# Clustered attention with a Mish feed-forward layer: another form for three tiny products, loads of V set apart, and a new order of issue

## The chip, the cores and the metric

One NeuronCore of a Trainium2 chip runs the whole kernel. The metric is the device time of one execution in microseconds (us). The engines are TensorE (PE, matrix products), VectorE (DVE), ScalarE (ACT), GpSimd (POOL) and the queue of SyncE (SP), which issues most DMAs. Each engine works through its own instructions in order, and so does each queue.

## The reference: attention inside clusters, then a feed-forward layer

```python
q_n, k_n, c_n = (t / (norm(t) + 1e-6) for t in (q, k, centroids))
q_assign = argmax(einsum('bhsd,hcd->bhsc', q_n, c_n))   # 16 clusters
k_assign = argmax(einsum('bhsd,hcd->bhsc', k_n, c_n))
mask   = q_assign[:, :, :, None] == k_assign[:, :, None, :]
scores = where(mask, q @ k.T / sqrt(64), -1e9)          # 768 x 768 per head
attn   = softmax(scores)
x = (attn @ v), heads side by side                       # (3072, 512)
h = x @ w_in                                             # (3072, 2048)
out = (h * tanh(softplus(h))) @ w_out                    # (3072, 512)
```

There are 4 batches of 8 heads, 768 positions and 64 numbers per head.

## The kernel before

**Units of work.** A unit `i` is one head and one block of 256 queries, so there are 96 units, 24 for each batch; each has two halves `a` of 128 queries. For a half, `scores(i, a)` (lines 625 to 643) writes 128 x 768 scores to PSUM, `rowmax` (L648, DVE) takes the row maxima, `expo` (L662, ACT) the exponentials with their sums, `total` and `recip` (L674, L682, DVE) the reciprocal sums. There are two PSUM buffers for scores, so `scores` of one half waits until `expo` two halves before has read its own.

From unit 24 on, the probabilities are split into two half-precision parts: `p_hi` on POOL (L700) and `p_lo` on DVE (L717: a scalar-tensor-tensor, which reads two tensors from SBUF). `ptrans` (L733) transposes both by DMA on SP's queue, and `pv(m, part)` (L753, PE) multiplies the transposed probabilities of units 2m and 2m+1 with V. In the first 24 units PE transposes instead (L710), and V is used in full precision. `pv_out` and `x_lo` (L790, L814) bring the result to SBUF. `prep_hi` and `prep_lo` (L484, L487, L500; POOL) split the next head's q and k; `prep_lo` is a tensor-tensor.

**Feed-forward layer.** `m1` (L832 to L834), `e_mish` (L843, ACT), `e_gh` (L849, POOL), `e_gl` (L857, DVE) and `m2` (L873 to L875) run between the units of the batch that follows. Weights are loaded, scaled and split in the first 200 us (`w_load`, `w_low`, `w_f32`, `w_sq`, `w_hi`, `w_lo`).

**V and the scales.** V of batch b comes in four loads of 384 KB, `v_load(b, hp)` (L356, SP's queue), one per two heads. The loads and the split copies that `v_high` (L441, POOL) and `v_split` (L430, DVE) make share six buffers. `v_sq` (L368, ACT) squares each load for the batch's scale. A scale per batch is a power of two in a 128 x 1 column. `moe_scale_h(b)` (L447, L451) and `moe_scale_o(b)` (L459) multiply such columns on DVE, once per batch: twelve instructions in all, each on 128 x 1 numbers.

**What sets the order.** Every operation has a due time, made from the tables `T`, `N` and, one operation at a time, `SHIFT` (line 41). The planner (line 51) issues them by due time; `pl.after` in an operation first issues what it needs. All engines and SP's queue then keep that order, so an operation that waits holds whatever stands behind it on its engine or queue.

Of the kernel before, what the change touches and what calls it, by code (L numbers as in the profile page):

```python
# [72 lines left out]
def tile_clustered_attention_mish_ffn(  # L73
# [1327 lines left out]
    ('load', 0): -8.977,  # L1401
    ('load', 1): -9.331,
    ('load', 2): -6.804,
    ('load', 3): -5.619,
    'prep_hi': -3.465,
    'prep_lo': 0.23,
    'copy_t': -2.657,
    'copy_z': -2.269,
    'copy_a': -1.819,
    'hot_copy': -1.496,  # L1410
    'copy_b': -0.963,
    'assign_mm': -3.945,
    'assign_turn': -4.253,
    'assign_max': -4.024,
    'assign_hot': -0.819,
    'assign_back': -3.241,
    'assign_put': 1.027,
    'assign_stg': -2.392,
# [11 lines left out]
    'expo': 3.967,  # L1430
    'total': 8.731,
    'recip': 0.231,
    'p_hi': 3.325,
    'p_lo': 4.618,
    'ptrans': 0.814,
    'pv': [3.293, 11.429, 2.946],
    'pv_out': 7.913,
    'x_lo': 2.788,
    'm1': [0.115, 0.891, 1.22, 1.321],
    'e_mish': [7.039, 1.656],  # L1440
    'e_gh': [1.735, 2.085],
    'e_gl': [1.659, 2.922],
    'm2': [5.418, 4.348, 9.247, 4.881, 6.012, 11.05, 9.763, 4.899, 4.471, 5.038, 4.927, 19.283, 4.585, 5.024, 8.214, 4.739],
    'm_out': -0.192,
    'm_store': -0.425,
# [10 lines left out]
    ('qk_load', 1): 0.234, ('qk_load', 2): -8.097, ('qk_load', 3): 0.234, ('w_f32', 29): 0.56, ('w_low', 18): 0.238,
    ('w_low', 22): -0.008, ('pv', 5, 0): 0.03, ('w_low', 19): -0.127, ('pv_out', 10): 6.683, ('v_split', 1, 1): 0.53,
    ('recip', 8, 1): 0.054, ('recip', 1, 1): 0.532, ('w_hi', 10): -0.025, ('rowmax', 18, 1): 0.004,
    ('total', 7, 1): 0.207, ('w_low', 29): 0.382, ('w_low', 31): 0.354, ('total', 14, 1): 0.631, ('w_load', 0): 0.812,
    ('p_hi', 7, 0): 0.769, ('p_hi', 6, 1): -0.119, ('p_hi', 6, 0): 0.699, ('w_low', 21): 0.177, ('pv', 11, 0): 0.16,  # L1460
    ('w_f32', 17): -0.125, ('p_hi', 0, 0): -0.048, ('p_hi', 0, 1): -0.024, ('p_hi', 1, 0): -0.518,
    ('p_hi', 1, 1): -0.022, ('p_hi', 2, 0): -0.009, ('p_hi', 2, 1): -0.009, ('p_hi', 3, 1): -0.009,
    ('p_hi', 4, 1): -0.009, ('p_hi', 5, 1): -0.009, ('expo', 16, 1): 1.76, ('expo', 10, 1): -2.352,
    ('total', 11, 1): 2.886, ('p_lo', 20, 1): -0.478, ('p_lo', 21, 1): -0.062, ('p_lo', 22, 0): -0.335,
    ('p_lo', 22, 1): 0.969, ('p_lo', 23, 0): 0.043, ('p_lo', 23, 1): -0.838, ('p_lo', 24, 0): 2.44,
    ('p_lo', 24, 1): -0.148, ('p_lo', 25, 0): -1.539, ('p_lo', 25, 1): 1.12, ('p_lo', 26, 0): -0.755,
    ('p_lo', 27, 0): 0.027, ('scores', 29, 0): -0.211, ('rowmax', 21, 0): -0.09, ('v_sq', 0, 3): -0.653,
    ('w_load', 5): -0.533, ('e_gh', 0): -0.048, ('e_gh', 1): -0.048, ('copy_z', 9): -0.31, ('copy_z', 10): -0.069,
    ('copy_a', 8): -0.101, ('copy_a', 9): -0.042, ('w_low', 11): 0.141, ('rowmax', 5, 0): 0.002,
    ('v_load', 1, 3): -0.147, ('w_load', 6): 0.218, ('copy_z', 0): -0.468, ('prep_lo', 6): 6.254,  # L1470
# [5 lines left out]
    ('p_hi', 19, 1): 0.777, ('p_hi', 20, 0): 0.068, ('p_hi', 20, 1): 0.068, ('p_hi', 21, 0): 0.128,
    ('p_hi', 21, 1): 0.118, ('p_hi', 22, 0): 1.691, ('p_hi', 22, 1): 0.068, ('p_hi', 23, 0): 0.029,
    ('p_hi', 23, 1): 0.713, ('copy_b', 6): 0.145, ('copy_b', 7): 0.475, ('copy_b', 9): 0.03, ('centroids',): -0.486,
    ('x_lo', 12): 0.064, ('scores', 14, 0): 0.142, ('p_lo', 2, 1): -0.108, ('copy_t', 0): 0.443,
# [169 lines left out]
```

## Time and profile before

| | |
|---|---|
| median of 3 runs | 874.17 us (872.82 to 874.46) |
| the profiled execution, its own time | 873.21 us |
| its span (what the trace covers) | 871.5 us |
| PE busy | 839.7 us, 96% of the span |
| DVE, ACT, POOL busy | 698.3, 517.1, 437.9 us |
| granted TensorE clock | 1.0 (2.4 GHz) |

The profile gives, for one execution, busy time by engine and stretch, what ended each idle time, and every instruction with its start. 1.7 us of the profiled time lie outside the span.

### The profile page before, as it was taken

The page shows a single profiled execution, that of the slowest core. Times are in us where ns is not written, and L with a number is a line of the kernel's source. Part 1 is how long each engine was busy: PE and PEld are TensorE (multiplying, and loading weights), DVE is VectorE, ACT ScalarE, POOL GpSimd, SP SyncE. Part 2 cuts the span into 40 slices and gives each one's busy share as a digit, 9 for nine tenths or more (in the row PEclk, how much of TensorE's full clock was granted, in tenths as well). Part 3 has the DMA queues.
Part 4 walks back from the last instruction along what each step waited for, and adds up shares of the span by engine and source line. Part 5 has one row for each costly group of instructions (what it writes and reads, how often), then busy time and mean ns, then how long its engine had stood idle before and what let it go on. Part 6 is the DMA issues. An engine that isn't in the chain of part 4 may idle for free.

```text
span 871.5 us, 17410 instructions
## 1 busy us (share of the span) xinstructions
PE 839.7 (96%) x6671; PEld 608.6 (70%) x6671; DVE 698.3 (80%) x1178; ACT 517.1 (59%) x878; POOL 437.9 (50%) x410
## 2 busy tenths in 40 slices
PE   7899899889999999999999999999999999999998
PEld 3666666667767767776677767776776776777787
DVE  7889988889978878779978789779888776488831
ACT  6778977667547567456556666465565565245520
POOL 1463655486657646556567457466557543110000
PEclk9999999999999999999999999999999999999999
DMA  9755671289679897698679897987877976000000
GB/s 333 240 176 160 186 219 48 63 163 186 132 136 180 207 169 146 130 190 168 124 128 200 189 172 132 156 178 149 142 136 135 156 130 118 23 1 14 2 31 32
DMA packets 253060, 121.51 MB, mean 139 GB/s; under 512 B 230288, under 2 KB 230800, under 8 KB 252976
## 3 DMA queue, kind: packets, MB, share of 16 engines
q1 hardware_dynamic: 247632, 108.46, 59.4%
q10 hardware_dynamic: 5344, 11.93, 6.6%
q8 instruction: 53, 0.87, 0.4%
q14 instruction: 31, 0.25, 0.1%
HBM read 35.72 MB, written 6.29 MB: 48 GB/s over the span
## 4 chain that ended last, share of the span: by engine, by line
PE 72%; DVE 12%; DMA 5%; ACT 4%; POOL 3%; issue 3%; ACTq 0%; SPq 0%; DVEq 0%; POOLq 0%
PE o L753 9%; PE h L832 8%; PE h L834 8%; PE h L833 8%; PE O L873 7%; PE O L875 7%; PE O L874 7%; PE s L631 5%; PE s L636 5%; DVE m L648 4%; DMA pt<-hl 3%; DVE hl L717 2%; ACT p L662 2%; PE as L543 1%; PE q L710 1%
## 5 line engine op out<-in xcount | busy, mean ns | idle before, releaser
L662 ACT ACTIVATE p<-s,m 128x768 f32<-128x768 f32 x192 | 172.7, 899 | 174.2 <-DVE m L648 94.7
L700 POOL TENSOR_SCALAR hl<-p,l 128x768 f16<-128x768 f32 x144 | 172.7, 1200 | 149.3 <-DVE l L682 82.3
L648 DVE TENSOR_REDUCE m<-s 128x1 f32<-128x768 f32 x192 | 182.5, 952 | 39.7 <-PE s L636 36.2
L832 PE MATMUL h<-x,w 128*128 128x256 f16 x640 | 175.8, 275 | 2.5 <-ACT u L843 2.0
L717 DVE SCALAR_TENSOR_TENSOR hl<-p,l,hl 128x768 f16<-128x768 f32 x144 | 166.6, 1157 | 12.8 <-POOL hl L700 12.5
L833 PE MATMUL h<-x,w 128*128 128x256 f16 x640 | 174.4, 273 | 0.0
L834 PE MATMUL h<-x,w 128*128 128x256 f16 x640 | 174.4, 273 | 0.0
L631 PE MATMUL s<-A,B 128*128 128x384 f32 x384 | 118.9, 391 | 7.1 <-ACT p L662 6.1
L873 PE MATMUL O<-w,g 128*128 128x512 f16 x320 | 121.7, 380 | 0.0
L875 PE MATMUL O<-w,g 128*128 128x512 f16 x320 | 121.3, 379 | 0.0
L874 PE MATMUL O<-w,g 128*128 128x512 f16 x320 | 121.3, 379 | 0.0
L857 DVE SCALAR_TENSOR_TENSOR g<-u,mscg,g 128x512 f16<-128x512 f32 x80 | 91.6, 1145 | 34.2 <-POOL g L849 34.0
L849 POOL TENSOR_SCALAR g<-u,mscg 128x512 f16<-128x512 f32 x80 | 75.0, 940 | 65.7 <-ACT u L843 53.2
L636 PE MATMUL s<-Z,T 80*128 80x384 f32 x384 | 99.0, 339 | 2.2 <-DMA T<-stg 1.2
L832 PEld LDWEIGHTS <-w 128*128 128x128 f16 x768 | 75.1, 98 | 30.9 <-issue 19.7
L833 PEld LDWEIGHTS <-w 128*128 128x128 f16 x768 | 75.5, 98 | 13.9 <-issue 2.7
L753 PE MATMUL o<-pt,v 128*64 128x256 f16 x1296 | 79.1, 274 | 3.5 <-DMA pt<-hl 3.5
L834 PEld LDWEIGHTS <-w 128*128 128x128 f16 x768 | 75.1, 98 | 9.0 <-issue 0.2
L753 PEld LDWEIGHTS <-v 128*64 128x64 f16 x1296 | 68.4, 110 | 15.6 <-issue 11.7
L631 PEld LDWEIGHTS s<-A,B 128*128 128x128 f32 x384 | 61.3, 190 | 21.5 <-ACT p L662 9.4
L636 PEld LDWEIGHTS s<-Z,T 80*128 80x128 f32 x384 | 69.5, 189 | 3.0 <-DMA T<-stg 1.5
L500 POOL TENSOR_TENSOR B<-qk,A 128x768 fp32r<-128x768 f32 x30 | 61.6, 2052 | 0.6
(225 smaller groups left out, 1299.0 us busy)
## 6 DMA issues: line engine op xcount, KB each, us to landing
qk<-in_qk_dram SPq DMA_DIRECT2D x32, 384.0 KB, 4.8
stage<-in_w_in_dram SPq DMA_DIRECT2D x16, 512.0 KB, 6.6
stage<-in_w_out_dram SPq DMA_DIRECT2D x16, 512.0 KB, 4.4
vraw<-in_vP_dram SPq DMA_DIRECT2D x16, 384.0 KB, 6.2
T<-A ACTq DMA_DIRECT2D x30, 192.0 KB, 3.5
Z<-B SPq DMA_DIRECT2D x30, 192.0 KB, 3.0
B<-T ACTq DMA_DIRECT2D x28, 192.0 KB, 3.4
out_dram<-osb SPq DMA_DIRECT2D x20, 256.0 KB, 2.7
```

The lines of the kernel that those rows point to most:

```text
L631: nc.tensor.matmul(s[:, j, :384], st["B", n][:, q0 : q0 + P], st["A", n][:, j * 384 : (j + 1) * 384], start=True, stop=False,)
L636: nc.tensor.matmul(s[:, j, :384], st["T", n][: D + NCL, q0 : q0 + P], st["Z", n][: D + NCL, j * 384 : (j + 1) * 384], start=False, stop=True,)
L648: nc.vector.tensor_reduce(m, st["s", i, a][:, :, :384], axis=AX.XY, op=ALU.max, negate=True)
L662: nc.scalar.activation(p.rearrange("p (n x) -> p n x", n=2), st["s", i, a][:, :, :384], AF.Exp, bias=st["m", i, a], scale=1.0, accum_out=l,)
L717: nc.vector.scalar_tensor_tensor(t[:, 1], p, r, t[:, 0], op0=ALU.mult, op1=ALU.subtract)
L753: nc.tensor.matmul(o[s * D : s * D + D, :256], v if early else v[:, int(part == 1)], st["pt", 2 * m + s][:, :, c + (0 if early or part < 2 ...
L832: nc.tensor.matmul(o, wh, xh, start=(c == 0), stop=False)
L833: nc.tensor.matmul(o, wh, xl, start=False, stop=False)
L834: nc.tensor.matmul(o, wl, xh, start=False, stop=(c == 3))
L873: nc.tensor.matmul(o, gh, wh, start=(f == 0 and fi == 0), stop=False)
L874: nc.tensor.matmul(o, gh, wl, start=False, stop=False)
L875: nc.tensor.matmul(o, gl, wh, start=False, stop=(f == 7 and fi == 1))
```

## The change

Three things, in one diff. The products of columns in `moe_scale_h` and `moe_scale_o` become tensor-scalar instructions whose second column is a per-partition scalar operand. The loads of V of batches 2 and 3, whose four due times were equal, get due times of their own, from 0.6 to 6.6 units earlier. And the tables of due times are new: some 100 entries of `T` and `N`, and `SHIFT` grows from 705 entries, nearly all in the first 32 units, to 2,524 over the whole kernel. Shares, buffers and the work itself stay.

```diff
     def moe_scale_h(b):
         pl.after(scaled(b), ("w_scale", 0))
         t = sm.tile([P, 1], F32, tag="msch", name=f"msch{b}")
-        nc.vector.tensor_tensor(t, vst[b, "s"][:, 1:2], wst["s", 0][:, 1:2], op=ALU.mult)
+        nc.vector.tensor_scalar(t, vst[b, "s"][:, 1:2], wst["s", 0][:, 1:2], None, op0=ALU.mult)
         vst[b, "h"] = t
...
-        nc.vector.scalar_tensor_tensor(
-            g, vst[b, "s"][:, 0:1], 2.0**-14, wst["s", 0][:, 0:1], op0=ALU.mult, op1=ALU.mult
+        nc.vector.tensor_scalar(
+            g, vst[b, "s"][:, 0:1], wst["s", 0][:, 0:1], 2.0**-14, op0=ALU.mult, op1=ALU.mult
         )
...
     def moe_scale_o(b):
...
-        nc.vector.scalar_tensor_tensor(
-            t, vst[b, "h"], 2.0**14, wst["s", 1][:, 1:2], op0=ALU.mult, op1=ALU.mult
+        nc.vector.tensor_scalar(
+            t, vst[b, "h"], wst["s", 1][:, 1:2], 2.0**14, op0=ALU.mult, op1=ALU.mult
         )
...
 N = {
-    'v_load': 17.351,
+    'v_load': 16.905,
...
 SHIFT = {
+    ('v_load', 2, 0): -6.115, ('v_load', 2, 1): -4.014, ('v_load', 2, 2): -1.835, ('v_load', 2, 3): -0.275,
+    ('v_load', 3, 0): -6.141, ('v_load', 3, 1): -5.728, ('v_load', 3, 2): -2.038, ('v_load', 3, 3): -0.148,
...
```

(The last lines put together entries that stand apart in the new table.) Sorted by due time, each operation behind what it needs, the two tables give two orders. Counted in stretches of one operation, PE has 907 of which 789 keep their order among themselves; DVE 894 of 1,062, ACT 529 of 637, POOL 307 of 370, SP's queue 249 of 314. Nearly all moves are over at most four places. SP's queue around V of batch 2, before and after:

```
before: ... ptrans(39,1) hot_copy(14) ptrans(40,0) qk_load(18) v_load(2,0) v_load(2,1) v_load(2,2) v_load(2,3) ptrans(40,1) ptrans(41,0) ptrans(41,1)
after:  ... v_load(2,0) ptrans(34,0) ... v_load(2,1) ptrans(36,0) ... v_load(2,2) ptrans(38,0) ... ptrans(39,1) v_load(2,3) ptrans(40,0) qk_load(18) ptrans(40,1) qk_load(17) ptrans(41,0) ptrans(41,1)
```

## Rows read from the trace of the kernel before

**Rows 1.** Busy time by stretch: PE, PEld, DVE, ACT, POOL, clock, DMA share, GB/s.

```profile
0.00:200.00 200.00, 177.18 (x1335) 124.21 (x1336) 176.77 (x322) 148.86 (x282) 105.83 (x125) 1.00 0.62 177
200.00:750.00 550.00, 544.26 (x4371) 389.77 (x4369) 450.50 (x738) 322.28 (x526) 324.65 (x278) 1.00 0.82 153
```

**Rows 2.** Timeline of DVE around 161 us: start, us, line, operation.

```profile
161.20 2.11 DVE L447 TENSOR_TENSOR msch<-vs0r,ws0r 128x1 f32<-128x1 f32 x1
...
163.30 0.94 DVE L648 TENSOR_REDUCE m<-s 128x1 f32<-128x768 f32 x1
```

**Rows 3.** Timeline of POOL around 161 us.

```profile
161.16 2.13 POOL L349 TENSOR_TENSOR w<-w,w 128x1024 f16<-128x1024 f32 x1
```

**Rows 4.** Timeline of PE around 165 us; in brackets the idle time before.

```profile
165.39 0.62 PE L631 MATMUL s<-A,B 128*128 128x384 f32 x2 [1.00 <-ACT p L662]
```

**Rows 5.** One line, L447: its last execution, ns shortest, median, longest.

```profile
L447 DVE TENSOR_TENSOR msch<-vs3r,ws0r x1: 147/147/147, 733.9 to 733.9; 128x1 f32<-128x1 f32 x1
```

**Rows 6.** Timeline of DVE around 350 us.

```profile
350.03 1.76 DVE L447 TENSOR_TENSOR msch<-vs1r,ws0r 128x1 f32<-128x1 f32 x1
...
351.78 1.00 DVE L717 SCALAR_TENSOR_TENSOR hl<-p,l,hl 128x768 f16<-128x768 f32 x1
```

**Rows 7.** Timeline of POOL around 350 us.

```profile
349.53 2.24 POOL L500 TENSOR_TENSOR B<-qk,A 128x768 fp32r<-128x768 f32 x1
```

**Rows 8.** One line, L674: ns shortest, median, longest, and its shapes.

```profile
L674 DVE TENSOR_SCALAR l<-l x146: 133/144/585, 115.5 to 732.0; 128x1 f32<-128x1 f32 x144, 128x2 f32<-128x2 f32 x2
```

**Rows 9.** Timeline of DVE: the longest L674, and L610 with its column operand `put_b`.

```profile
71.95 1.02 DVE L610 TENSOR_SCALAR stg<-put,put_b 128x768 fp32r<-128x768 f32 x1
...
115.48 0.58 DVE L674 TENSOR_SCALAR l<-l 128x2 f32<-128x2 f32 x1
```

**Rows 10.** Timeline of POOL at the same two places.

```profile
70.83 1.82 POOL L500 TENSOR_TENSOR B<-qk,A 128x768 fp32r<-128x768 f32 x1
...
115.38 0.66 POOL L268 TENSOR_SCALAR stage<-stage 128x512 uint32<-128x512 uint16 x1 [2.50 <-DMA stage<-in_w_out_dram]
```

**Rows 11.** Timeline of DVE around 398 us.

```profile
398.45 0.56 DVE L459 SCALAR_TENSOR_TENSOR msco<-msch,ws1r 128x1 f32<-128x1 f32 x1
398.93 2.66 DVE L717 SCALAR_TENSOR_TENSOR hl<-p,l,hl 128x768 f16<-128x768 f32 x1
```

**Rows 12.** Timeline of POOL around 398 us.

```profile
398.09 0.91 POOL L700 TENSOR_SCALAR hl<-p,l 128x768 f16<-128x768 f32 x1 [0.41 <-DMA qk<-in_qk_dram]
398.97 1.81 POOL L500 TENSOR_TENSOR B<-qk,A 128x768 fp32r<-128x768 f32 x1
```

**Rows 13.** Timeline of PE around 404 us.

```profile
403.72 0.44 PE L631 MATMUL s<-A,B 128*128 128x384 f32 x1 [1.13 <-ACT p L662]
```

**Rows 14.** Timeline of SP's queue from 296 us: issue start and length.

```profile
296.58 1.86 SPq L356 DMA_DIRECT2D vraw<-in_vP_dram  x4
298.54 11.85 SPq L733 DMA_TRANSPOSE pt<-hl  x3
```

**Rows 15.** One line, L733: ns to issue one, and us from issue to landing.

```profile
L733 SPq DMA_TRANSPOSE pt<-hl x144: 1273/1450/5083, 170.1 to 738.3; - x144
...
DMA to landing us min/median/max: 3.6/3.9/11.4
```

**Rows 16.** Timeline of PE around 314 us and 507 us.

```profile
313.95 2.15 PE L753 MATMUL o<-pt,v 128*64 128x256 f16 x35 [1.70 <-DMA pt<-hl]
...
506.55 2.13 PE L753 MATMUL o<-pt,v 128*64 128x256 f16 x35 [0.87 <-DMA pt<-hl]
```

**Rows 17.** Timeline of ACT around 306 us: `expo(42, 1)` and one square of V (L368).

```profile
305.69 0.90 ACT L662 ACTIVATE p<-s,m 128x768 f32<-128x768 f32 x1 [1.40 <-DVE l L674]
...
306.58 0.83 ACT L368 ACTIVATE vq<-vraw 128x768 bf16<-128x768 f32 x1
```

**Rows 18.** Timeline of PE around 308 us: `scores(43, 1)`.

```profile
308.47 0.59 PE L631 MATMUL s<-A,B 128*128 128x384 f32 x2
```

**Rows 19.** Timeline of POOL at the start: its wait for the first weight load.

```profile
14.54 0.65 POOL L268 TENSOR_SCALAR stage<-stage 128x512 uint32<-128x512 uint16 x1 [11.85 <-DMA stage<-in_w_in_dram]
```

More of the change, by code (lines that the diff above doesn't have):

```diff
@@ L1400 @@
 N = {
[L1401 to L1418, printed above, removed]
-    'v_load': 17.351,
-    'v_sq': 18.178,
+    ('load', 0): -8.889,
@@ L1421 @@
+    ('load', 1): -9.421,
+    ('load', 2): -6.776,
+    ('load', 3): -5.617,
+    'prep_hi': -3.459,
+    'prep_lo': 2.58,
+    'copy_t': -2.7,
+    'copy_z': -2.222,
+    'copy_a': -1.917,
+    'hot_copy': -2.171,
+    'copy_b': -0.958,
+    'assign_mm': -0.311,
+    'assign_turn': -4.276,
+    'assign_max': -3.984,
+    'assign_hot': -1.184,
+    'assign_back': -3.243,
+    'assign_put': 2.145,
+    'assign_stg': -2.374,
+    'v_load': 16.905,
+    'v_sq': 18.324,
     'v_scale': 21.77,
-    'v_max': 20.441,
+    'v_max': 18.893,
@@ L1423 @@
     'v_pair': 10,
-    'v_high': 30.994,
-    'v_low': 27.359,
+    'v_high': 35.746,
+    'v_low': 27.356,
     'v_d': 4.243,
-    'E': [0.372, 0.793, 1.234, 1.538],
-    'scores': 1.895,
+    'E': [0.384, 0.793, 1.234, 1.538],
+    'scores': 1.991,
     'rowmax': -0.3,
[L1430 to L1445, printed above, removed]
[3 rows of a table removed]
+    'expo': 3.904,
+    'total': 6.224,
+    'recip': 0.225,
+    'p_hi': 13.925,
+    'p_lo': 5.917,
+    'ptrans': 0.818,
+    'pv': [4.606, 11.977, 4.089],
+    'pv_out': 7.569,
+    'x_lo': 2.785,
+    'm1': [0.153, 0.664, 1.179, 1.534],
@@ L1456 @@
[L1456 to L1470, printed above, removed]
@@ L1476 @@
[L1476 to L1479, printed above, removed]
-    ('v_high', 0, 2): 0.19, ('assign_back', 2): -0.035, ('rowmax', 15, 0): -0.209, ('x_lo', 16): 1.015,
@@ new lines @@
+    ('v_sq', 1, 3): 0.833, ('total', 18, 0): 2.103, ('prep_lo', 0): -2.242, ('qk_load', 11): 3.653,
+    ('total', 10, 0): 0.442, ('v_max', 0): -0.228, ('v_high', 1, 0): -2.376, ('w_sq', 0): 0.247, ('w_f32', 7): 0.065,
+    ('w_spread', 1): -0.025, ('total', 6, 0): 8.03, ('w_sq', 30): 0.554, ('w_load', 30): -0.049,
+    ('expo', 4, 1): 0.197, ('prep_hi', 4): 0.128, ('w_load', 11): 1.202, ('rowmax', 4, 0): -0.131,
+    ('w_load', 15): 1.893, ('p_lo', 16, 1): 2.687, ('pv_out', 11): 2.399, ('total', 17, 0): 1.438,
@@ new lines @@
+    ('w_load', 3): -0.119, ('rowmax', 26, 1): -0.136, ('total', 17, 1): -0.068, ('expo', 23, 0): -0.177,
+    ('w_lo', 10): 1.862, ('pv_out', 15): 0.043, ('assign_mm', 3): 3.013, ('p_lo', 12, 1): -0.291,
+    ('total', 20, 1): 1.672, ('e_gh', 2): 0.174, ('w_sq', 27): 3.242, ('w_sq', 6): 2.585, ('copy_b', 0): 0.938,
+    ('scores', 4, 0): 0.267, ('w_hi', 1): 0.386, ('hot_copy', 11): 0.48, ('prep_hi', 0): -0.059, ('w_load', 8): 2.33,
+    ('ptrans', 26, 1): -0.044, ('prep_hi', 3): -7.162, ('hot_copy', 3): -0.623, ('w_sq', 18): 0.052,
@@ new lines @@
+    ('recip', 14, 0): 3.049, ('p_lo', 0, 0): 1.604, ('pv', 2, 0): 0.149, ('recip', 18, 1): 0.19,
+    ('hot_copy', 2): -0.623, ('w_sq', 20): -0.066, ('expo', 27, 1): 1.155, ('recip', 21, 0): -0.45,
+    ('w_sq', 2): 0.175, ('w_low', 26): 0.071, ('v_sq', 0, 2): -4.969, ('v_sq', 0, 1): -2.465, ('qk_load', 4): -0.754,
+    ('total', 14, 0): 3.363, ('w_abs', 2): -0.415, ('p_hi', 4, 0): -1.782, ('v_max', 1): -0.256, ('w_sq', 14): -0.011,
+    ('m1', 1, 1): 7.158, ('scores', 2, 0): 0.036, ('e_gl', 2): -0.031, ('scores', 20, 1): -0.191,
@@ new lines @@
+    ('expo', 21, 0): -0.373, ('p_hi', 8, 1): -0.033, ('rowmax', 25, 1): 0.005, ('prep_hi', 11): 0.002,
+    ('m1', 2, 1): -0.133, ('hot_copy', 4): 4.62, ('w_abs', 12): -0.053, ('pv_out', 7): -0.009, ('w_sq', 3): 0.003,
+    ('p_lo', 0, 1): -0.39, ('p_lo', 1, 1): -0.88, ('ptrans', 14, 0): -0.084, ('ptrans', 8, 1): 0.097,
+    ('w_abs', 21): -0.076, ('w_low', 28): 0.355, ('ptrans', 20, 1): 0.016, ('w_abs', 19): -1.925, ('x_lo', 17): 1.106,
+    ('expo', 20, 0): 0.06, ('prep_lo', 4): 0.501, ('prep_lo', 7): 1.348, ('recip', 9, 0): -2.297,
@@ new lines @@
+    ('p_hi', 24, 1): 0.826, ('p_hi', 25, 1): 0.716, ('p_lo', 28, 0): 0.229, ('p_lo', 28, 1): 2.539,
+    ('v_split', 0, 3): -0.06, ('v_split', 0, 1): -0.016, ('v_load', 1, 1): 0.317, ('ptrans', 19, 1): 0.105,
+    ('scores', 17, 1): 0.001, ('x_lo', 13): 0.266, ('p_hi', 9, 0): -0.021, ('pv_out', 19): 0.371,
+    ('pv_out', 17): 0.019, ('w_hi', 9): 4.053, ('w_low', 16): -0.221, ('w_lo', 3): 0.014, ('assign_hot', 2): 0.072,
+    ('rowmax', 22, 1): -0.123, ('expo', 15, 0): -0.084, ('qk_load', 7): 0.323, ('w_abs', 22): -0.017,
@@ new lines @@
+    ('w_load', 22): -0.096, ('w_load', 24): -0.157, ('w_load', 28): -0.132, ('w_load', 29): 0.147,
+    ('p_lo', 66, 1): 0.59, ('assign_mm', 7): 0.135, ('ptrans', 75, 0): 0.032, ('pv_out', 36): -0.397,
+    ('pv', 43, 2): -1.313, ('rowmax', 66, 1): 0.008, ('p_hi', 32, 1): 0.998, ('expo', 35, 1): 1.018,
+    ('e_gh', 28): 1.449, ('p_hi', 51, 1): 2.014, ('e_mish', 52): 0.736, ('prep_lo', 17): 0.295, ('p_hi', 75, 1): 1.23,
+    ('e_gl', 21): -0.151, ('m2', 7, 1, 2): 1.916, ('rowmax', 68, 1): 0.088, ('expo', 83, 0): -0.074,
@@ new lines @@
+    ('recip', 41, 1): -0.126, ('recip', 42, 0): -0.195, ('expo', 38, 0): -3.223, ('w_sq', 23): -0.061,
+    ('p_hi', 78, 1): 0.367, ('e_gh', 62): -0.118, ('copy_z', 24): -0.069, ('recip', 48, 0): 0.022,
+    ('copy_z', 22): 0.058, ('expo', 56, 0): 2.663, ('w_sq', 26): 0.023, ('pv', 27, 2): 0.704,
+    ('rowmax', 70, 1): -0.075, ('rowmax', 47, 0): 0.054, ('total', 58, 1): 1.04, ('v_sq', 2, 1): 0.282,
+    ('v_sq', 2, 2): 0.558, ('v_sq', 2, 3): -0.295, ('p_lo', 78, 0): 0.053, ('recip', 46, 1): -0.293,
@@ new lines @@
+    ('rowmax', 40, 0): 0.014, ('copy_a', 24): 0.5, ('e_gh', 47): 0.622, ('expo', 34, 0): -0.034,
+    ('expo', 35, 0): 0.507, ('p_hi', 66, 0): -0.02, ('rowmax', 43, 0): 0.056, ('copy_b', 22): 0.378,
+    ('copy_b', 23): 0.083, ('copy_b', 24): 0.244, ('p_lo', 56, 1): -2.619, ('m2', 1, 0, 7): 0.144,
+    ('scores', 35, 0): -1.684, ('m2', 0, 1, 3): 0.012, ('m2', 2, 0, 5): -0.008, ('m2', 2, 1, 2): 0.185,
+    ('m2', 2, 1, 4): 0.012, ('m2', 2, 1, 5): -0.022, ('m2', 2, 1, 7): -0.022, ('m2', 3, 0, 0): -0.496,
@@ new lines @@
+    ('p_lo', 45, 1): 0.111, ('p_lo', 46, 0): 0.111, ('e_mish', 63): 0.059, ('p_hi', 33, 0): 0.625,
+    ('m1', 18, 1): -0.083, ('w_sq', 25): -0.016, ('assign_mm', 5): -0.066, ('pv_out', 73): 0.47,
+    ('rowmax', 84, 0): 0.032, ('total', 66, 1): 2.555, ('scores', 35, 1): 0.383, ('pv_out', 78): -0.277,
+    ('hot_copy', 19): 0.394, ('expo', 47, 1): 3.19, ('expo', 40, 0): -0.022, ('x_lo', 51): 0.239,
+    ('w_low', 12): 0.007, ('expo', 81, 0): 0.021, ('scores', 54, 1): -0.851, ('e_gh', 24): 0.151,
@@ new lines @@
+    ('e_mish', 6): 0.186, ('pv', 37, 0): 1.212, ('rowmax', 57, 1): -0.002, ('v_load', 2, 1): -4.014,
+    ('ptrans', 64, 0): 0.031, ('m1', 42, 0): 0.129, ('prep_hi', 19): 1.374, ('total', 49, 1): -0.327,
+    ('copy_a', 3): 0.197, ('scores', 12, 1): 1.219, ('ptrans', 63, 1): 0.154, ('x_lo', 23): -0.326,
+    ('expo', 30, 0): 0.594, ('rowmax', 77, 1): -0.265, ('p_hi', 55, 0): -0.459, ('p_lo', 55, 0): 1.045,
+    ('m2', 6, 1, 6): 0.007, ('m2', 2, 1, 3): 0.582, ('prep_lo', 10): 0.005, ('m1', 57, 1): -0.233,
```

794 lines of the change are left out of this document (600 added, 194 removed), and 36 rows, old and new, of tables (N, SHIFT).

## Prediction

> **What bounds the kernel now.** First the page's busy times, which the table above gives: PE at 96% of the span, so what can be won without less PE work is a few per cent. Then busy time by stretch, to see where PE's idle time lies: 22.8 us in the first 200 us (200 less 177.18), 5.7 us between 200 and 750 us (550 less 544.26) [rows 1]. In the first stretch DVE is busy for 176.77 of 200 us and no engine is full: PE waits for chains that go through all engines. In the second PE is the bound, with a few separate holes. So I look for single holes whose cause the diff touches. For that I took PE's timeline, and from each hole went back to what held the engine that released PE.
>
> **Part 1, the column products.** An L447 on 128 x 1 numbers takes 0.147 us when nothing is in its way [rows 5], but 2.11 us at 161.20 [rows 2], 1.76 us at 350.03 [rows 6] and the same a batch later. Each of these ends when a tensor-tensor on POOL ends: 161.16 + 2.13 = 163.29 [rows 3] against 163.31, and 349.53 + 2.24 = 351.77 [rows 7] against 351.79. DVE's two-tensor read waits for POOL's. The new form reads one tensor and a column. Does that still wait? L674, a tensor-scalar on 128 x 1, has a median of 144 ns over 146 executions and a longest of 585 [rows 8]; the longest is one of its two 128 x 2 executions [rows 9], beside a POOL instruction from 115.38 to 116.04 [rows 10]. L610 has a column operand and kept its 1.02 us from 71.95 while POOL's tensor-tensor ran from 70.83 to 72.65 [rows 9, 10]; it reads PSUM, though. So I take 0.147 us for each of the twelve new instructions. Bounds for one: 0.147 us, and the 2.11 us of today if it waits as before. What each saving is worth, place by place:
>
> At 161 us the instruction behind it is a row maximum [rows 2] that starts with no idle time before it, so that its scores were ready by then. If they were ready 2 us before (PE went on to other work in between), it starts up to 2.0 us sooner; its exponential follows, and that frees the scores buffer for which PE waits 1.00 us at 165.39 [rows 4]. Gain 1.00 us; less if the next buffer becomes the wait, more if the chain keeps its lead (bounds 0 and 1.96, what the instruction itself saves).
>
> At 350 us, and a batch later, nothing: right behind it stands `p_lo`, L717, which reads two tensors itself and would wait for the same POOL instruction to the same 351.77 [rows 6, 7]; PE has no hole there. If a one-tensor instruction stood there instead, the gain would be in DVE's slack.
>
> At 398 us the scalar-tensor-tensor of `moe_scale_o(1)` takes 0.56 us: it waits for POOL's `p_hi`, which ends at 399.00 [rows 11, 12]. `p_lo(53,0)` comes next, at 398.93, just too late: POOL's `prep_lo` starts at 398.97, and `p_lo` takes 2.66 us where an undisturbed one takes 1.00 [rows 6, 11, 12]. The row maximum behind it is late, the exponential too, and PE stands for 1.13 us before 403.72 [rows 13] and, one batch later at the same place, for as long again. With the new form `p_lo` is at the door from about 398.5 and is the one that goes when `p_hi` ends, as `moe_scale_o` was; it then ends near 400.0 instead of 401.59, 1.6 us sooner, more than the hole. The new order keeps `p_hi`, `prep_lo` on POOL and `moe_scale_o` ahead of `p_lo` on DVE. Gain 2 x 1.13 = 2.26 us (bounds 0, if `prep_lo` still goes first, and 2.26).
>
> A rule bears on who goes first. The Trainium skill, SBUF — State Buffer, section "SBUF: two separate sides", has the shared port pair as an exclusive lock that whichever starts first keeps for a whole instruction; it does not say who of two waiting gets it. By that rule alone the 2.26 us would be open; by the rows of that place the instruction that waits on DVE went at once when `p_hi` ended.
>
> **Part 2, the loads of V.** At 296.58 four loads of 384 KB go onto SP's queue in 1.86 us; the three transposes behind them take 11.85 us to issue, to 310.39 [rows 14], where one takes a median of 1.45 us, and landing takes 3.9 us from its issue [rows 15]. At that median the third would start at 301.4, or when its data come, and land 3.9 us later; PE wanted it at 312.25 and stood for 1.70 us to 313.95 [rows 16]. So it would be in time even if its data came up to 6.9 us after 301.4. The same burst of batch 3 costs 0.87 us at 506.55 [rows 16]. In the new order the loads of batch 2 have at least three transposes between one and the next, loads 0 and 1 of batch 3 have one; between the first and last transposes for that `pv` two loads of q and k remain where five transfers of 384 KB stood. Each load moved is one DMA of 384 KB, past up to 22 entries of SP's queue; on no other queue does it move. Its buffer is free at its new place (six buffers, at most six in use by the new order), and the last one of each batch still stands behind `v_split`, as today, so I price these waits at nothing. The first readers, the squares on ACT, move too: four in a row, 4 x 0.83 = 3.3 us [rows 17] and their read-outs, some 4 us, between the exponentials of `expo(42, 0)` and `(42, 1)`, where one stood at a time; in batch 3 three stand in a row. What covers it is that `scores(42, 0)` is put ahead of a whole `pv`, 2.1 us of PE [rows 16], so that its exponential comes earlier and the squares fall into ACT's idle time; I cost them at nothing. With that cover gone, `expo(42, 1)`, which now ends at 306.6, ends 4 us later, and PE, which takes `scores(43, 1)` at 308.5 [rows 18], stands for 2.1 us. A load in front of other transposes can delay them by the time of one load, a quarter of the burst; there the transposes reach PE 4.3 us or more after their issue against the 3.9 us needed, and the loads stand ahead of early ones of a group of four. Gain 1.70 + 0.87 = 2.57 us (bounds 0 and 2.57).
>
> **Part 3, the rest of the order.** About one operation in six swaps places with neighbours. No work is added, and PE's own work by operation is the same. From the trace I can't price a swap: each may open a hole of about 1 us, as those before 165 and 404 us [rows 4, 13], or close one. In the second stretch only 5.7 us of holes exist, of which 4.83 are counted above. In the first stretch 21.8 us stay, so up to some 4 us could go if a fifth of them closed, and as much could come. I take 0, between equal bounds.
>
> **Sum.** 1.00 + 2.26 + 2.57 = 5.83 us. The profiled execution, 873.21 us, would take 867.4 us; its span 865.7. The median of the runs is 0.96 us above the profiled one, so the forecast for it is 874.17 - 5.83 = 868.3 us.
>
> **The rivals.**
> 1. *More holes close.* The new order also shortens the first 200 us, by 2 to 4 us: 864 to 866 us. For it: 21.8 us of idle PE there. Against: that stretch's holes come from chains through four engines, with DVE at 88%. Chance 0.14.
> 2. *The new form waits as well.* Part 1 gives nothing: 874.17 - 2.57 = 871.6 us. For it: the 128 x 2 executions of the same form do wait [rows 8 to 10]. The Trainium skill, VectorE: DVE Perf Modes, section "Mode 2×_2P", has a tensor-scalar on SBUF use both read ports when its outermost dimension is even. Against: 128 x 1 never did, and one element can't be shared out. Chance 0.08.
> 3. *The transposes crowd themselves.* Not V but the transposes and copies around 302 us make the landing late; the waits at 314 and 507 us stay: 874.17 - 3.26 = 870.9 us. For it: the second and third transpose were slow when the loads were issued 4 us before. Chance 0.08.
> 4. *The gain is given back.* The squares of V hold ACT in both batches, 2 x 2.1 = 4.2 us: 868.3 + 4.2 = 872.5 us; with one or two holes of about 1 us more from swaps, 873 to 875. For it: the row maximum of `scores(42, 0)` must come as early as PE's part of it for the cover to hold. Against: ACT stands idle for some 4 us there now. Chance 0.11.
> 5. *Slower: a weight load comes late.* In SP's order four loads of weights now go ahead of `w_load(8)`, two of them from far behind, while POOL, DVE and PE still take block 8 before block 9. PE's queue stands at `w_sq(8)`, near 48 us, until it lands. What a late weight load can cost is the 11.85 us that POOL stood at the start [rows 19]: 868.3 + 11.85 = 880.2 us at worst. It decides from 5.83 + 1.75 = 7.6 us on. Against: SP hands out those loads from 24 us on, some 20 us before their use. Chance 0.07.
>
> **How the numbers follow.** Forecast 0.52; the rivals as above. 0.2% of 874.17 is 1.75 us, about what a measurement of this kernel can tell from no change. Under 872.4 us lie the forecast and rivals 1, 2 and 3: 0.82. Rival 4 is the same, 0.11; rival 5 slower, 0.07. The range runs from rival 1's lower end, 864.0, to 873.0: above it lie most of rival 4 and rival 5, below it what the bounds add up to at their best; together under 0.2.
>
> **What would show it.** L447, L451 and L459 at 0.15 us each; no hole of 1 us in PE after the first `moe_scale_h`, none after `moe_scale_o(1)` and `(2)`, with `p_lo` there near 1.0 to 1.5 us; the transposes behind V's loads at about 1.5 us an issue and no wait of PE for `pt` near 310 and 500 us; PE's idle time between 200 and 750 us near 1 us, and in the first 200 us near 22. Wrong would be: the same PE idle time after 200 us, L459 still at 0.5 us, or more than 25 us idle in the first 200.

## The result, and the profile after

| | before | after |
|---|---|---|
| median | 873.79 us (872.82 to 874.46, 6 runs) | 864.24 us (861.37 to 867.35, 6 runs) |
| the profiled execution, its span | 873.21, 871.5 us | 866.38, 864.6 us |
| PE busy | 839.7 us, 96% | 838.4 us, 97% |
| DVE busy | 698.3 us | 690.2 us |

The ratio is 0.9898, with a 95% interval of 0.9877 to 0.9918: 9.5 us faster by the medians. The runs of after spread over 6.0 us, those of before beside them over 1.6 (869.45 to 877.79 us in a later comparison with 29 of them); the profiled execution of after is one of its slower ones, 6.8 us under that of before. So a single profile of after must be read with care, and a second one follows in run 6.

Busy time by stretch, after (columns as in [rows 1]: time of the stretch, then busy time of PE, PEld, DVE, ACT and POOL, the granted clock, the DMA share and GB/s; PE's idle time is the first figure less the second):

```profile
0.00:200.00 200.00, 182.05 (x1394) 130.10 (x1395) 179.21 (x332) 153.80 (x290) 111.55 (x129) 1.00 0.65 183
200.00:750.00 550.00, 544.98 (x4361) 393.14 (x4359) 443.18 (x733) 319.12 (x520) 313.24 (x276) 1.00 0.82 151
```

PE's idle time in the first 200 us fell from 22.8 to 17.95 us, where the prediction expected 1.0 us to go. From 200 to 750 us it fell only from 5.7 to 5.0 us, where 4.8 us were expected to go. The holes that the prediction named did go. DVE and POOL around the two products of `moe_scale_h(2)`, after (answers to [rows 2, 6]), from the timelines of the two engines:

```profile
539.36 0.20 DVE L447 TENSOR_SCALAR msch<-vs2r,ws0r 128x1 f32<-128x1 f32 x1
539.48 0.20 DVE L451 TENSOR_SCALAR mscg<-vs2r,ws0r 128x1 f32<-128x1 f32 x1
...
538.54 1.81 POOL L500 TENSOR_TENSOR B<-qk,A 128x768 fp32r<-128x768 f32 x1
```

Both DVE instructions start and end while POOL's tensor-tensor runs, from 538.54 to 540.35: the new form doesn't wait. The Trainium skill, VectorE: DVE Perf Modes, section "Mode 2×_2P", splits a tensor-scalar's operand in half along its outermost dimension to use both read ports. From this it may be inferred that a 128 x 1 column leaves nothing to split; the 0.20 us of this trace agree, but do not show that this is the reason. Undisturbed, the new form is slower than the old one: 0.20 us (727.0 us, the fourth batch) against 0.147 [rows 5].

The place of the holes at 404 us, after: DVE and POOL near 390 us, and PE's next scores (answers to [rows 11 to 13]).

```profile
389.69 0.20 DVE L459 TENSOR_SCALAR msco<-msch,ws1r 128x1 f32<-128x1 f32 x1
390.35 0.43 DVE L814 SCALAR_TENSOR_TENSOR x<-o,x 64x256 f16<-64x256 f32 x1 [0.47 <-ACT x L790]
390.81 1.15 DVE L717 SCALAR_TENSOR_TENSOR hl<-p,l,hl 128x768 f16<-128x768 f32 x1
...
389.37 1.78 POOL L700 TENSOR_SCALAR hl<-p,l 128x768 f16<-128x768 f32 x2
391.12 2.51 POOL L500 TENSOR_TENSOR B<-qk,A 128x768 fp32r<-128x768 f32 x1
...
394.55 0.69 PE L631 MATMUL s<-A,B 128*128 128x384 f32 x2
```

`p_lo` waits from 390.81 until POOL's `p_hi` ends at 391.15 and goes next; `prep_lo` is the one that waits now (2.51 us for 1.81). PE has no hole in front of its scores. But the new order has also put an `x_lo` (L814) between the product and `p_lo`, which matters in runs 4 and 7.

The loads of V and PE at `pv(20)` and `pv(32)`, after (answers to [rows 14, 16]):

```profile
286.66 0.94 SPq L356 DMA_DIRECT2D vraw<-in_vP_dram  x1
...
298.75 3.13 SPq L733 DMA_TRANSPOSE pt<-hl  x2
...
305.98 0.74 PE L753 MATMUL o<-pt,v 128*64 128x256 f16 x10
...
499.97 2.16 PE L753 MATMUL o<-pt,v 128*64 128x256 f16 x36
```

One load stands there instead of four, and neither `pv` waits. What took the place of these holes shows in PE's waits by line (engine, line, what it waited for: us in total, times, longest), before and then after:

```profile
PE s L631 <- ACT p L662: 6.1, 7, 1.1
PE q L710 <- ACT p L662: 4.5, 8, 0.9
PE gram L296 <- DVE w L276: 4.3, 5, 1.7
PE o L753 <- DMA pt<-hl: 3.5, 4, 1.7
```

```profile
PE o L753 <- DMA pt<-hl: 5.8, 6, 1.6
PE gram L296 <- DVE w L276: 3.1, 4, 1.4
PE s L631 <- ACT p L662: 2.5, 3, 2.0
PE q L710 <- ACT p L662: 2.4, 5, 0.8
```

The waits for exponentials and weights are down by 6.9 us in these lines, those for transposed probabilities (`pt`) up by 2.3 us, although the two that the prediction named are gone. The largest new ones, on PE's timeline:

```profile
464.50 0.74 PE L753 MATMUL o<-pt,v 128*64 128x256 f16 x10 [1.38 <-DMA pt<-hl]
...
594.87 2.15 PE L753 MATMUL o<-pt,v 128*64 128x256 f16 x35 [1.62 <-DMA pt<-hl]
```

### The profile page after: what moved, and what is told of

Same layout as the page of the kernel before. It is cut to its first block, busy times and chain, and to the rows that moved or that the text cites. A ratio compares the mean times of both kernels' runs of the same rounds, so it can differ in the third digit from the quotient of the medians.

```text
span 864.6 us, 17394 instructions
## 1 busy us (share of the span) xinstructions
PE 838.4 (97%) x6671; PEld 613.0 (71%) x6671; DVE 690.2 (80%) x1178; ACT 517.5 (60%) x878; POOL 431.4 (50%) x410
## 4 chain that ended last, share of the span: by engine, by line
PE 73%; DVE 13%; DMA 6%; ACT 3%; issue 2%; POOL 2%; ACTq 0%; SPq 0%; DVEq 0%; POOLq 0%
PE o L753 9%; PE h L832 8%; PE h L834 8%; PE h L833 8%; PE O L873 7%; PE O L875 7%; PE O L874 7%; PE s L631 5%; PE s L636 5%; DVE m L648 4%; DMA pt<-hl 4%; DVE hl L717 2%; PE as L543 1%; DMA stage<-in_w_out_dram 1%; DVE w L347 1%
## 5 line engine op out<-in xcount | busy, mean ns | idle before, releaser
L700 POOL TENSOR_SCALAR hl<-p,l 128x768 f16<-128x768 f32 x144 | 167.4, 1165 | 171.9 <-DVE l L682 77.3
L717 DVE SCALAR_TENSOR_TENSOR hl<-p,l,hl 128x768 f16<-128x768 f32 x144 | 172.2, 1200 | 11.8 <-POOL hl L700 11.3
L849 POOL TENSOR_SCALAR g<-u,mscg 128x512 f16<-128x512 f32 x80 | 77.3, 969 | 66.3 <-ACT u L843 56.8
L857 DVE SCALAR_TENSOR_TENSOR g<-u,mscg,g 128x512 f16<-128x512 f32 x80 | 82.9, 1037 | 24.4 <-POOL g L849 24.2
L843 ACT ACTIVATE u<-h,msch 128x512 f32<-128x512 f32 x80 | 52.2, 686 | 29.0 <-PE h L834 21.9
```

The source lines that it names most:

```text
L717: nc.vector.scalar_tensor_tensor(t[:, 1], p, r, t[:, 0], op0=ALU.mult, op1=ALU.subtract)
```

## The experiments

All gains are against runs of before on the same chip: 873.36 us for the first four, 874.19 for the next four, 873.65 for the last. A gain in us is one less the ratio, times that figure; the ratio comes from all the runs, so the gain differs by up to some 1.1 us from the difference of the medians. In hybrids (runs 3 to 5 and 9 to 12) an order is a list of all operations; each operation's due time is its place in that list, and the list is put together from those of before and after.

**Run 1, the new form alone.** Edit: in before, the three products of the diff above (L447, L451, L459) in their new form; nothing else.

> The kernel before with the new form of the twelve column products alone; order and loads as before. Theory A (Part 1 of the prediction): L447 takes 0.2 us at 161 and 350 us, PE's hole of 1.00 us before 165 goes, the two of 1.13 us near 404 and 597 go: 3.26 us faster, ratio 0.9963. Rival B: the form alone moves nothing, because the p_lo behind it waits for the same POOL instruction and prep_lo still goes ahead of it; the holes near 404 and 597 stay at about 1.1 us: 0 to 1 us faster, ratio 0.9989 to 1.000.

Measured: 871.08 us, ratio 0.9961 (0.9942 to 0.9981), 3.4 us (1.7 to 5.1) faster, as theory A has it. DVE and POOL at 398 us:

```profile
397.82 0.21 DVE L459 TENSOR_SCALAR msco<-msch,ws1r 128x1 f32<-128x1 f32 x1
397.96 1.22 DVE L717 SCALAR_TENSOR_TENSOR hl<-p,l,hl 128x768 f16<-128x768 f32 x1
...
397.47 0.91 POOL L700 TENSOR_SCALAR hl<-p,l 128x768 f16<-128x768 f32 x1 [0.42 <-DMA qk<-in_qk_dram]
398.34 2.51 POOL L500 TENSOR_TENSOR B<-qk,A 128x768 fp32r<-128x768 f32 x1
```

This is the prediction's mechanism step by step: the product no longer waits for `p_hi`, `p_lo` is at the door when `p_hi` ends at 398.38, and it ends at 399.18 where [rows 11] had 401.59. The holes near 404 and 597 us are gone, and so is the one after the first `moe_scale_h`. A new wait for `pt`, 1.62 us near 524 us, takes some of it back in this profile. The Trainium skill, SBUF — State Buffer, section "SBUF: two separate sides", calls the shared ports a lock that one instruction keeps to its end; the 2.51 us of `prep_lo`, where 1.81 is undisturbed [rows 12], agree.

**Run 2, the loads of V alone.**

```diff
+SHIFT.update({('v_load', 2, 0): -6.561, ('v_load', 2, 1): -4.46, ('v_load', 2, 2): -2.281, ('v_load', 2, 3): -0.721,
+              ('v_load', 3, 0): -6.587, ('v_load', 3, 1): -6.174, ('v_load', 3, 2): -2.484, ('v_load', 3, 3): -0.594})
```

> The kernel before with new due times for the eight loads of V of batches 2 and 3 alone. Theory A (Part 2): the waits for pt of 1.70 us at 314 and 0.87 us at 507 go and none comes: 2.57 us faster, ratio 0.9971. Rival B: a load in front of earlier transposes makes new waits for pt of about the same sum: within 1 us of before, ratio 0.9989 to 1.0011.

Measured: 871.14 us, ratio 0.9978 (0.9960 to 0.9996), 1.9 us faster. The interval takes in 2.57 us and reaches into rival B's; the trace decides: both waits for `pt` are gone and none has come near them.

```profile
200.00:750.00 550.00, 547.12 (x4395) 392.21 (x4393) 449.65 (x738) 322.57 (x527) 324.43 (x278) 1.00 0.81 153
```

PE stands for 2.88 us in this stretch (550 less 547.12) where it stood for 5.74 [rows 1]: 2.86 us less.

**Run 3, the early order alone.**

```diff
+order = after_order[:after_order.index(('scores', 32, 0))]
+order += [op for op in before_order if op not in order]
```

> The order of after up to scores(32,0), from there that of before; old form of the column products. Theory A: the term that was taken as 0 (Part 3) is won in the first 200 us: unit 32 starts 4.95 us sooner in after's profile, and nothing later gives it back: 4 to 6 us faster, ratio 0.9931 to 0.9954. Rival B: most of that lead hangs on what is issued later and is lost at the seam: under 2 us faster, ratio over 0.9977.

Measured: 867.36 us, ratio 0.9926 (0.9899 to 0.9953), 6.5 us (4.1 to 8.8) faster. This is theory A, a little above its upper end, and the largest single part of the gain, with the old form and V's loads as before. The pair of holes of Part 1 (1.13 us each, now at 396 and 589 us) and the waits at `pv(20)` and `pv(32)` (1.62 and 1.10 us) are all still there. But the third place of Part 1 is not: under this order the old form no longer waits at the first `moe_scale_h`.

```profile
156.51 0.24 DVE L447 TENSOR_TENSOR msch<-vs0r,ws0r 128x1 f32<-128x1 f32 x1
```

It took 2.11 us in before [rows 2]; here POOL's next tensor-tensor starts at 156.71 us, after the product. So the 6.5 us can hold the 1.00 us that the prediction gave to the new form at this place.

**Run 4, the late order alone.** As run 3 with before and after exchanged: the order of before up to `scores(32, 0)`, that of after behind it, with the loads of V apart.

> The order of before up to scores(32,0), from there that of after, the loads of V of batches 2 and 3 apart among it; old form of the column products. Theory A: what the profile of after gained behind unit 32, 6.8 less 4.95 = 1.9 us in that execution and 2.7 us more in the median: 1.9 to 4.6 us faster, ratio 0.9947 to 0.9978. Rival B: the closed holes are exchanged for new waits for pt one for one: within 1 us, ratio 0.9989 to 1.0011.

Measured: 872.60 us, ratio 0.9982 (0.9963 to 1.0000), 1.6 us faster: between the theories, and undecided by time alone. This is no more than the loads alone gave in run 2, although the holes near 404 and 597 us are gone too; they went without the new form. DVE and POOL at 398 us in this run:

```profile
397.55 0.61 DVE L459 SCALAR_TENSOR_TENSOR msco<-msch,ws1r 128x1 f32<-128x1 f32 x1
398.22 0.43 DVE L814 SCALAR_TENSOR_TENSOR x<-o,x 64x256 f16<-64x256 f32 x1
398.69 1.15 DVE L717 SCALAR_TENSOR_TENSOR hl<-p,l,hl 128x768 f16<-128x768 f32 x1
...
397.24 1.79 POOL L700 TENSOR_SCALAR hl<-p,l 128x768 f16<-128x768 f32 x2
398.99 2.52 POOL L500 TENSOR_TENSOR B<-qk,A 128x768 fp32r<-128x768 f32 x1
```

The old product still waits (0.61 us), but it stands one place earlier, `x_lo` runs behind it, and `p_lo` is at the door in time for the end of `p_hi` at 399.03. So form and order close the same holes, and their gains don't add. That the time shows nothing of it has a second reason in this profile. Between 200 and 750 us PE stands for 2.0 us, 0.9 less than in run 2, but before 200 us, where the order is that of before, the granted clock fell twice, by its row:

```profile
0.00:200.00 200.00, 178.10 (x1324) 125.88 (x1326) 175.23 (x318) 146.94 (x278) 103.99 (x124) 0.98 0.62 175
```

In the profile of run 2 it stayed at 1.00.

**Run 5, the combination.** The order of run 3, the loads of run 2, the form of run 1; behind `scores(32, 0)` the order of before but for V's loads.

> The order of after up to scores(32,0), behind it the order of before, with the new form of the column products and with the loads of V of batches 2 and 3 apart. Theory A: the parts lie in different stretches and add, and after's own late order is not needed: 6 us from the first 200 us, 2.3 us from the holes near 404 and 597, 2 to 2.6 us from the waits for pt near 312 and 505: 10 to 11 us faster than before, ratio 0.9874 to 0.9886, and at least as fast as after. Rival B: after's late order carries a share that this leaves out: 6 to 8 us faster, ratio 0.991 to 0.993.

Measured: 862.24 us, ratio 0.9856 (0.9833 to 0.9879), 12.6 us faster, and faster than after in the same comparison (run 6). This is theory A, above its upper end. The three parts summed are 3.4 + 1.9 + 6.5 = 11.8 us, or about 10.8 if the 1.00 us at the first `moe_scale_h` is in two of them; both lie inside the interval (10.6 to 14.6 us), so within the noise the parts add. Its busy time from 200 to 750 us:

```profile
200.00:750.00 550.00, 549.44 (x4405) 394.58 (x4404) 447.30 (x737) 320.81 (x524) 321.90 (x276) 1.00 0.79 151
```

PE stands for 0.56 us there. This is the "near 1 us" that the prediction expected of after.

**Run 6, after once more.** No edit.

> After as it is, for a second profile beside the others. Theory A: its late waits for pt (1.59 us at pv(30), 1.84 at pv(38), 0.7 to 1.0 at pv(34) and pv(37)) come from its order and stand in this execution too, each within 0.5 us; the time is 9 to 10 us under before, ratio 0.9885 to 0.990. Rival B: they are chance of one execution: at least two of the four are gone, and with them the time is 2 to 3 us lower than in the first profile.

Measured: 865.26 us, ratio 0.9905 (0.9879 to 0.9931), 8.3 us faster; the profiled execution took 863.30 us, 3.1 less than the first one. Rival B for the waits at `pv(30)`, `pv(37)` and `pv(38)`: they are gone or under 0.4 us. Only that at `pv(34)` stays (0.92 us over the usual time). What differs is the queue. The same three transposes in the same order on SP's queue, in the first profile of after and then in the second:

```profile
582.11 9.57 SPq L733 DMA_TRANSPOSE pt<-hl  x3
```

```profile
581.26 6.87 SPq L733 DMA_TRANSPOSE pt<-hl  x3
```

In the first PE waits 1.62 us for them, in the second not at all. So these waits aren't fixed by the order. They are most of the difference between the two profiles: PE's idle time between 200 and 750 us is 5.0 us in the first and 1.7 in the second. How much of after's spread over other executions is theirs isn't shown.

**Run 7, after with the old form.** Edit: the three products of the diff put back.

> After with the old form of the twelve products. Theory A: the new order has closed the holes near 404 and 597 by itself (the late order alone showed neither), and the form is worth 0 to 1 us there: ratio to before 0.989 to 0.9905. Theory B (Part 1 as predicted, in this order too): 3.26 us slower than after, ratio 0.9928, with the two holes of 1.1 us back.

Measured: 863.29 us, ratio 0.9872 (0.9848 to 0.9896). It isn't told apart from after (run 6: the intervals overlap), and theory B's 0.9928 lies outside. In after's order the new form is worth nothing that shows; `p_lo` at that place takes 1.15 us, as in run 4, and the holes near 404 and 597 us don't come back. In this third profile of after's order the waits for `pt` are 1.4 us in all, and PE stands for 1.5 us between 200 and 750 us.

**Run 8, after with V's loads together.** Edit: all eight `v_load` of batches 2 and 3 due at the times of before, four and four equal.

> After with the four loads of V of batch 2 due at one time again, and those of batch 3. Theory A (Part 2): the waits for pt of about 1.9 us at pv(20) and 1.1 at pv(32) come back: 2 to 3 us slower than after, ratio to before 0.991 to 0.993. Rival B: the transposes around them stand earlier in the new order and are in time all the same: 0 to 0.8 us slower than after, ratio 0.989 to 0.990.

Measured: 869.89 us, ratio 0.9942 (0.9924 to 0.9959): 0.9942 less 0.9905 is 0.0037, 3.2 us slower than after. This is theory A, above its upper end, but only for batch 2: at `pv(32)` no wait for `pt` came back, and PE stands there instead for 1.19 us, at 502 us, for a load of q and k; whether V's loads delay that one isn't shown. SP's queue and PE at `pv(20)`:

```profile
290.40 1.84 SPq L356 DMA_DIRECT2D vraw<-in_vP_dram  x4
292.35 2.83 SPq L733 DMA_TRANSPOSE pt<-hl  x1
...
297.75 6.24 SPq L733 DMA_TRANSPOSE pt<-hl  x2
...
307.75 3.31 PE L753 MATMUL o<-pt,v 128*64 128x256 f16 x35 [2.48 <-DMA pt<-hl]
```

The wait is 2.48 us, longer than the 1.70 of before, and then the 35 products take 3.31 us where they take 2.15 [rows 16]. Busy time by stretch tells why (the sixth figure, behind POOL, is the granted clock):

```profile
306.00:308.00 2.00, 0.24 (x5) 0.25 (x7) 1.90 (x2) 0.00 (x0) 0.84 (x3) 1.00 0.88 271
308.00:310.00 2.00, 2.00 (x29) 1.79 (x25) 1.51 (x2) 1.67 (x2) 1.88 (x2) 0.64 1.15 216
310.00:312.00 2.00, 2.00 (x17) 0.90 (x17) 0.58 (x3) 1.67 (x4) 0.22 (x2) 0.50 1.28 256
312.00:314.00 2.00, 2.00 (x22) 0.69 (x15) 1.10 (x2) 0.38 (x1) 1.66 (x2) 1.00 0.36 78
```

After the hole the clock is at its lower level, 1.2 GHz (0.50), and back at 2.4 GHz by 312. Between 308 and 312 us this costs 2 x 0.36 + 2 x 0.50 = 1.7 us of full-speed work, about as much again as the wait that the loads cause in before. A second fall in this execution, near 176 us, comes long before V's loads, so the 3.2 us need not all be theirs: by the mean granted clock of the six runs, 0.997 against 0.998 in run 6, some 0.9 us (an estimate: 0.001 of the 868 us).

**Runs 9 and 10, the early order in two halves.** Run 9: the order of after up to `scores(20, 0)`, then that of before. Run 10: that of before up to `scores(20, 0)`, after's to `scores(32, 0)`, then that of before.

> The order of after up to scores(20,0), from there that of before; old form of the products. Theory A: the gain of the early order (6 us) is spread over both halves; unit 20 starts 1.6 us sooner in after's first profile, and PE's loss between 25 and 50 us, where weights arrive, is 1.0 to 1.8 us in every profile with after's early order and 2.6 to 5.4 in those with that of before: 1.5 to 3 us faster, ratio 0.9966 to 0.9983. Rival B: nothing of it is here, within 0.8 us, ratio over 0.9991.

> The order of before up to scores(20,0), after's from there to scores(32,0), and that of before behind it; old form of the products. Theory A: the larger share of the early gain, the holes between 140 and 200 us: 3 to 4.5 us faster, ratio 0.9949 to 0.9966. Rival B: this stretch gives under 1.5 us, ratio over 0.9983, and the first 20 units carry the gain.

Measured: 870.37 us, ratio 0.9971 (0.9951 to 0.9991), and 870.45 us, ratio 0.9971 (0.9950 to 0.9993): 2.5 us each (0.8 to 4.3 and 0.6 to 4.4). This is theory A for the first; the second gives less than A says, with A's 0.9966 inside the interval. The early gain is no single hole but lies over both halves, though these intervals leave the shares open.

**Runs 11 and 12, two tries at a better order.** The largest hole left stands in front of `scores(27, 0)`. Run 11 is run 5 with one operation moved on DVE, run 12 adds three on PE:

```diff
 order = [... p_hi(24,1),
+         rowmax(26,0),
          e_gl(0), ... p_lo(25,0), ...
-         rowmax(26,0),
# run 12 also:
+         scores(28,0), m1(4,1), m1(4,0),
          x_lo(24) with pv(12), ...
```

> The combination of the run before, with one DVE instruction moved: the row maximum of scores(26,0), ready at 169.4 us, goes ahead of e_gl(0), which waits for POOL to 170.88, and of p_lo(25,0). Theory A: PE's hole of 2.29 us ahead of scores(27,0), near 172 us, closes and nothing takes its place: 1.5 to 2.3 us faster than the combination, ratio to before 0.983 to 0.984. Rival B: the wait goes to pv(12), whose last transpose waits for p_lo(25,1), only 0.9 us sooner than now: 0 to 1 us faster than the combination, ratio 0.9845 to 0.9856, with a wait for pt over 2 us at pv(12).

> As the run with the moved row maximum, and on PE scores(28,0) and m1(4) go ahead of pv(12). Theory A: both the hole of 2.29 us and the wait of 1.3 us for pt at pv(12) are covered: 2.5 to 3.5 us faster than the combination, ratio to before 0.9816 to 0.9827. Rival B: scores(28,0) then waits for expo(27,0), and the time is that of the run with the row maximum alone, within 0.5 us.

Measured for run 11: 860.61 us, ratio 0.9850 (0.9825 to 0.9875), not told apart from run 5, as rival B has it. PE's timeline, run 5 and then run 11:

```profile
175.66 0.62 PE L631 MATMUL s<-A,B 128*128 128x384 f32 x2 [2.04 <-ACT p L662]
182.61 2.15 PE L753 MATMUL o<-pt,v 128*64 128x256 f16 x35 [1.09 <-DMA pt<-hl]
```

```profile
175.69 0.58 PE L636 MATMUL s<-Z,T 80*128 80x384 f32 x2 [0.92 <-DMA Z<-stg]
182.67 2.15 PE L753 MATMUL o<-pt,v 128*64 128x256 f16 x35 [1.51 <-DMA pt<-hl]
```

The hole of 2.04 us became one of 0.92 us, for another transfer, and the next wait grew from 1.09 to 1.51, less than the 2 us that rival B named.

Measured for run 12: 863.60 us, ratio 0.9888 (0.9864 to 0.9911): neither theory; its median lies 3.0 us above that of run 11. The wait at `pv(12)` is gone, but the operations that now cover it are those that used to stand in front of `scores(29, 0)`:

```profile
190.22 1.01 PE L631 MATMUL s<-A,B 128*128 128x384 f32 x2 [2.90 <-ACT p L662]
```

```profile
190.00:192.00 2.00, 1.78 (x6) 1.41 (x7) 1.27 (x5) 1.48 (x4) 1.29 (x2) 0.50 1.14 208
192.00:194.00 2.00, 2.00 (x11) 1.42 (x10) 1.97 (x5) 1.54 (x5) 0.50 (x1) 0.50 1.10 217
194.00:196.00 2.00, 2.00 (x10) 1.53 (x8) 0.95 (x2) 1.94 (x2) 0.74 (x1) 0.50 0.05 10
```

The second fence is busy time by stretch of the same run. That hole, 2.90 us in one piece, left the clock at 0.50 for the 6 us shown, which costs some 3 us. The exponential that ends it starts at the same time in both runs (189.17 and 189.31 us); PE only came to it sooner.

## Why the prediction was right, and where it was not

The forecast was 868.3 us with a range of 864.0 to 873.0; 864.24 lies just inside. Faster was right; the term that missed is Part 3, and so what happened is mostly rival 1, which had a chance of 0.14. That the time lies inside the range is partly luck. The early order gave more than rival 1's 2 to 4 us, and the time stayed above 864.0 in part because Part 1 did not come on top of the new order; run 5, where the parts add, lies below it at 862.24 us.

**Part 1, right for the form alone, wrong for the change as a whole.** The forecast was 3.26 us, and the form alone gave 3.4 us (run 1). The step to `p_lo` going first is shown by its rows. The prediction also said that `moe_scale_o` keeps its place ahead of `p_lo`, but missed three things: for `moe_scale_o(2)` it doesn't (`p_lo(77, 0)` now stands in front of it); a shift of one `x_lo` closes the hole near 404 us even with the old form (runs 4 and 7), and the one near 597 us goes in these runs too; and the early order lets the old form pass at the first `moe_scale_h` (run 3). In after this term is therefore not additional. The twelve instructions take 0.20 us instead of the 0.147 assumed, in DVE's slack.

**Part 2, right.** The forecast was 2.57 us; the loads gave 1.9 us alone, with 2.86 us less PE idle time in that trace, and 3.2 us when taken out of after (run 8). The larger figure there includes a lower clock behind the wait, a cost that the prediction didn't have. Rival 3, that the transposes crowd themselves, fell in run 2. Something like it stands at the new wait at `pv(38)`, where three transposes with no load of V among them took 9.57 us; it comes and goes between executions.

**Part 3, mis-sized.** "I take 0, between equal bounds" of some 4 us. Up to `scores(32, 0)` the new order gives 6.5 us (4.1 to 8.8 by its interval), in two halves of 2.5 us (runs 9, 10). Rival 1 had this at 2 to 4 us. The reason given against it, that the holes there come from chains through four engines, was no obstacle: the waits for exponentials and weights all shrink a little. Which swaps do it is not shown. Behind `scores(32, 0)`, beyond the two holes of Part 1 that it closes as the form does, the new order wins nothing that shows and perhaps loses. Run 5, with the order of before there, is 0.0049 or 4.3 us ahead of after (the intervals touch at 0.9879), but only 0.0016 or 1.4 us ahead of run 7, which has the same order as after (the intervals overlap). Of that difference the traces show PE's idle time between 200 and 750 us: 0.6 us in run 5; 1.7 and 1.5 us in runs 6 and 7, 5.0 us in the first profile of after. So about 1 us of loss is seen, and more in an execution with the waits for `pt`.

**The other rivals.** Rival 2 fell with the rows at 539 us. Rival 4 needed squares of V of batches 2 and 3 that hold ACT; in after, PE's waits for exponentials in front of scores are 2.5 us in all, 2.0 of them in one at 176 us, before any of these squares. Rival 5 didn't come: no hole at `w_sq(8)` in after.

**The signs to look for** were right for the products and the two pairs of holes, and wrong for the totals: idle PE time in the first 200 us was to stay near 22 us and was 17.95, and between 200 and 750 us it was to be near 1 us and was 5.0 in one profile of after, 1.7 in the other (548.31 of 550 us busy).

So after's 9.5 us are, as the runs taken one at a time add up: about 6.5 from the early order (with the hole at the first `moe_scale_h`) and about 4 from the two pairs of late holes, less some 1 us that the late order may give back. The first and the last were Part 3, taken as 0.

## What to carry to other kernels

When a diff edits an instruction and reorders around it, ask of each hole whether the order alone would close it: two cures of one hole don't add, and only undoing one of them shows which is at work. Where many waits through several engines make up the idle time, a new order can win in one stretch and nothing, or less, in another, so try its stretches apart: here the early part of the new order with the late part of the old one, the new form and V's loads apart beat both kernels (862.24 us). A wait that one profile shows on a loaded DMA queue should be looked for in a second execution before it is explained.

## What the runs showed of the hardware that was not expected

**A hole can cost more than its length.** In run 1 PE stood for 1.44 us before 32.08 us and the granted clock fell:

```profile
30.00:32.00 2.00, 0.65 (x5) 0.33 (x3) 1.42 (x2) 2.00 (x5) 1.84 (x3) 1.00 0.78 220
32.00:34.00 2.00, 1.92 (x8) 1.28 (x10) 0.79 (x1) 0.49 (x1) 1.84 (x3) 0.68 0.13 28
34.00:36.00 2.00, 2.00 (x11) 1.24 (x8) 1.23 (x9) 1.04 (x3) 0.67 (x2) 0.50 0.92 292
```

In before the hole at this place was 1.18 us and the clock stayed at 1.00. It is no matter of length alone: the hole of 2.04 us near 174 us left the clock at 1.00 in after and at 0.50 from 176 to 178 us in run 8. In run 8 the two falls, here and at `pv(20)`, cost some 1.7 us each. Such falls are frequent: 1.7 us are 0.002 of an execution, and the mean granted clock is below 1.00 in 38 of the 63 runs of before that were measured beside the experiments. The 25 at 1.00 took 872.8 us on average, the 16 at 0.996 or less 874.6 us. An order can bring them on: run 11 had a clock of 1.00 in five of six runs, run 12 in none. When the clock falls in a given execution these runs don't tell.

**The issue of a DMA transpose isn't a fixed cost.** Three of them took 9.57 us on SP's queue in one execution of after and 6.87 us in another, with the same entries around them. What makes the difference isn't shown.
